# A hand-written order of the first units, written anew: which engine rounds which weight piece, and where each step stands

## The chip, the cores and the metric

One core of a Trainium2 chip. The metric is the device time of one execution in microseconds; the median of the runs is taken. The core's engines are TensorE (PE in the profile, PEld its weight loads), VectorE (DVE), ScalarE (ACT), GpSimd (POOL) and SyncE (SP), which issues most DMAs. Each runs its own instructions in the order in which the kernel wrote them and waits on semaphores for the others.

## The reference

A gated linear recurrence over 768 steps (4 batches, 8 heads, 48 features), and behind it a feed-forward layer with the maximum of three products:

```python
f = 1.0 / (1.0 + np.exp(-f_logit))
for t in range(S):
    state = f[:, :, t, :, None] * state + np.einsum('bhd,bhe->bhde', k[:, :, t], v[:, :, t])
    y[:, :, t] = np.einsum('bhd,bhde->bhe', q[:, :, t], state)
...
x = np.ascontiguousarray(attn_out.transpose(0, 2, 1, 3)).reshape(B * S, H * D)
h = np.maximum(np.maximum(x @ w1, x @ w2), x @ w3)
return (h @ w_out).astype(np.float32)
```

x is 3072 x 384; w1, w2 and w3 are 384 x 768, w_out is 768 x 384. The weights come as float64.

## The kernel before, in words

**Units.** The recurrence is cut into chunks of 64 steps. A unit is one chunk of two batches, all heads: 128 tokens, 24 units in all. Four units make a group of 512 tokens, for which the feed-forward layer then runs, as filler work on TensorE between the steps of later units. Units 0 to 3 and most of 4 and 5 go by the list of steps this case is about; from there on a loop issues them.

**One unit, by the names of the list** (the number behind a name is the unit): sT transposes the gates' logits on TensorE (L302), sA takes their sigmoid on ScalarE (L1039), s scans them backward on VectorE (L340, and a reciprocal, L343). kT transposes k, kM multiplies it by the scan (kh, VectorE, L1044). pS is the forward scan (L1051), qT and qM the same for q (qh, L1056). KT and KC turn kh back and copy it out (ks; L1062 on TensorE, L1065 on ScalarE). pP makes the scores within the chunk (a, L1072), pM masks them (L1076). v multiplies them by the values (y, L422), yP adds the part from the carried state (L1083, L1088), yC copies y out (o, L1093, ScalarE). SP makes the sums for the next state (L1102), SN adds them to it (L457 on ScalarE for units 0 and 1, L459 on VectorE behind that), c and kE scale and keep it on GpSimd. xP and xC turn the outputs into the layer's input xT (L1109, L1110). LD and LV load a unit's tensors.

**Weights.** They arrive as 24 pieces of 128 x 384 (LW loads so many; DMA at L222): piece n < 18 is column block j = n // 3 of w1, w2 or w3 by n % 3, the last six are w_out. Each piece is rounded from float64 to float32 in three steps. RB (`round_begin`) runs on ScalarE: the low word's part (rest_bits, L248) and, unless the piece is in BY_VECTOR, two activations that prepare the sign (top_bits, L244 and L245). RM (`round_merge`) runs on VectorE: one instruction (L262), or for a piece in BY_VECTOR two (a tensor_scalar at L259 and L260). RA (`round_add`) adds both parts on GpSimd (L269). top_bits has four buffers and rest_bits three, so RB of a piece waits for RA of the piece three before it.

**Differences.** w2 and w3 are replaced by w2 - w1 and w3 - w1 (`apart`, L766): AP n does it for piece n on GpSimd, AV n on VectorE. A product needs its piece's difference.

**The layer in the list.** F issues a product on TensorE (three matrix products into a bank, L553; 256 columns wide for the first twelve, 512 behind that, where it takes two F), E what takes it out of the bank: for w2 a copy on ScalarE (hm, L822), for w3 the maximum on VectorE (L824). There are two such banks (p). A bank is also taken by the transposes kT and qT of units 0 to 2, by yP's one-column product, by TP and by B (a filler product). TP j turns a piece of w1 on TensorE (L1115), TC j copies it back (L1117).

**What sets the order.** HEAD is a string of such steps. Each engine gets its instructions in the order of the string; nothing reorders them. So moving a step moves it on its own engine, and moves its place among the banks and buffers that it takes.

Of the kernel before, what the change touches and what calls it, by code (L numbers as in the profile page):

```python
# [55 lines left out]
def kernel(  # L56
# [33 lines left out]
    def fast():  # L90
        ctx = ExitStack()
        with ctx:
# [133 lines left out]
            def words(n):  # L226
                w = raw[n].rearrange("p (c two) -> p c two", two=2)
                return w[:, :, 0], w[:, :, 1]
# [2 lines left out]

            BY_VECTOR = (2, 3, 7, 9, 10, 12, 13, 15, 17)
            tops = keep.tile([128, 4, PIECE], FP32, name="top_bits")
            rests = keep.tile([128, 3, PIECE], FP32, name="rest_bits")

            def round_begin(n):
                if n in raw:
                    lo, hi = words(n)  # L240
                    top = tops[:, n % 4].bitcast(U32)
                    if n not in BY_VECTOR:

# [11 lines left out]
            def round_merge(n):  # L255
                if n in raw:
                    (top, rest), (_, hi) = halfway[n], words(n)
                    if n in BY_VECTOR:
                        nc.vector.tensor_scalar(top, hi, 3, 0x3FFFFFF8, op0=ALU.logical_shift_left, op1=ALU.bitwise_and)  # L259
# [757 lines left out]
            with tc.manual_schedule():  # L1017
# [11 lines left out]
                load_weights(6)  # L1029
                load_v(3)  # L1030
                xT = x_tiles[0]
                HEAD = """sT0 sA0 kT0 sT1 s0 kM0 kE0 kT1 qT0 pS0 sA1 s1 qM0 sT2 pP0 kM1 KT0 LD4 sA2 KT1 qT1 KC0 pS1 pM0 KC1 SP0 v0 qM1 SN0 pP1 kE1 s2 pM1 kT2 yP0 qT2 RB0 kE2 yC0 kM2 sT3 sA3 LW2 v1 RB1 KT2 KC2 LV4 c2 xP0 pS2 SP1 qM2 RB2 RM0 RM1 SN1 RA0 xC0 s3 RM2 pP2 RA1 B1 yP1 kT3 AP1 yC1 xP1 kM3 KT3 xC1 RB3 KC3 pS3 LW2 B1 kE3 F pM2 RM3 RB4 RA2 RM4 RA3 E qT3 v2 SP2 RB5 RB6 qM3 RA4 SN2 RB7 c3 AV2 AV4 pP3 yP2 RM5 F RM6 pM3 yC2 E RA5 RM7 F LW2 AV5 xP2 RA6 v3 LW2 xC2 TP0 SP3 E RB8 F RA7 AP7 TC0 SN3 RM8 LD5 TP1 E RB9 sT4 sA4 RA8 yP3 RM9 LV5 TC1 yC3 F AV8 kT4 xP3 E xC3 RA9 s4 RB10 kE4 TP2 kM4 F TC2 c4 RM10 E RB11 RB12 qT4 F RA10 LW2 RM11 E pS4 RA11 LW2 F RB13 E RM12 F qM4 RM13 E RB14 RA12 F RM14 E KT4 KC4 RB15 RA13 AP13 LW2 sT5 F RB16 LD6 E sA5 AV10 AV11 F LW2 E pP4 RA14 F RM15 RB17 F AV14 RA15 s5 kT5 RM17 LV6 pS5 TP3 RM16 qT5 RB18 RM18 LW2 E LW2 LW2 LW2 kE5 RA16 TC3 RA17 F F kM5 E RB19 LW2 c5 RA18 pM4 LW2 qM5 F AP16 S6"""
                BUDGET = -1146.666666666667
                held = {}
                first = ffn_first(xT)
# [84 lines left out]
                def RA(n):  # L1120
# [7 lines left out]
                           F=lambda n: next(first), E=lambda n: next(first))  # L1128
                for step in HEAD.split():
                    name = step.rstrip("0123456789")  # L1130
# [102 lines left out]
    def general():  # L1233
# [5 lines left out]
        with ctx:  # L1239
# [194 lines left out]
            for u in range(NU):  # L1434
# [5 lines left out]
                if u % GRP == GRP - 1:  # L1440
                    ffn(u // GRP, xT)

    fast()
    n_low = nc.values_load(low[0:1, 0:1], min_val=0, max_val=256)

# [32 lines left out]
```

## Time and profile before

| | us |
|---|---|
| median of 3 runs | 404.47 (404.35 to 405.72) |
| the profiled execution | 404.57 |
| its span, first to last instruction | 402.9 |
| TensorE busy | 388.4 |
| VectorE busy | 302.2 |
| GpSimd busy | 249.4 |
| ScalarE busy | 175.2 |

A row of the timeline gives an instruction's start and its length in us, the engine, the line, the operation, what it writes and reads, and in brackets how long the engine sat idle before and who ended that. TensorE executes one matrix product as two instructions, so a product F of three shows as x6. Instructions that follow each other overlap a little at their ends: a step of 0.68 is followed by the next after about 0.6.

### The profile page before, as it was taken

The page shows a single profiled execution, that of the slowest core. Times are in us where ns is not written, and L with a number is a line of the kernel's source. Part 1 is how long each engine was busy: PE and PEld are TensorE (multiplying, and loading weights), DVE is VectorE, ACT ScalarE, POOL GpSimd, SP SyncE. Part 2 cuts the span into 40 slices and gives each one's busy share as a digit, 9 for nine tenths or more (in the row PEclk, how much of TensorE's full clock was granted, in tenths as well). Part 3 has the DMA queues.
Part 4 walks back from the last instruction along what each step waited for, and adds up shares of the span by engine and source line. Part 5 has one row for each costly group of instructions (what it writes and reads, how often), then busy time and mean ns, then how long its engine had stood idle before and what let it go on. Part 6 is the DMA issues. An engine that isn't in the chain of part 4 may idle for free.

```text
span 402.9 us, 11666 instructions
## 1 busy us (share of the span) xinstructions
PE 388.4 (96%) x4658; PEld 339.2 (84%) x4658; DVE 302.2 (75%) x582; ACT 175.2 (43%) x419; POOL 249.4 (62%) x279
## 2 busy tenths in 40 slices
PE   4879999999999999999999999999999999999995
PEld 3768855569998889998889988899988899988995
DVE  6998998999989998997998997998995450002600
ACT  2675666513234432345532444523355325586120
POOL 2176546889997697296677277657477850535700
PEclk9999999999999999999999999999999999999999
DMA  8999886867564776676645476734572003452002
GB/s 166 238 298 278 208 236 81 193 88 125 97 94 90 112 146 145 115 112 83 123 122 92 65 115 86 167 68 80 79 158 86 0 19 92 129 146 70 2 20 63
DMA packets 181610, 47.21 MB, mean 117 GB/s; under 512 B 160496, under 2 KB 179248, under 8 KB 181552
## 3 DMA queue, kind: packets, MB, share of 16 engines
q1 hardware_dynamic: 177536, 45.52, 55.3%
q10 hardware_dynamic: 4016, 0.91, 1.1%
q8 instruction: 37, 0.61, 0.6%
q14 instruction: 21, 0.17, 0.1%
HBM read 37.75 MB, written 4.72 MB: 105 GB/s over the span
## 4 chain that ended last, share of the span: by engine, by line
PE 90%; DVE 3%; SPq 3%; DMA 2%; ACT 1%; issue 1%; POOL 0%; POOLq 0%
PE p L900 20%; PE p L640 18%; PE tr L900 16%; PE tr L640 14%; PE p L553 6%; PE y L426 3%; PE p L800 3%; PE y L515 2%; PE a L407 2%; PE a L444 2%; SPq L178 1%; SPq L164 1%; DMA raw<-in_moe_w_dram 1%; DMA placed<-in_moe_w_dram 1%; PE y L422 1%
## 5 line engine op out<-in xcount | busy, mean ns | idle before, releaser
L393 DVE STREAM_TRANSPOSE ks<-kh 32x128 f32<-32x128 f32 x256 | 77.4, 302 | 11.5 <-POOL kh L351 7.4
L900 PE MATMUL tr<-xT,placed 128*128 128x256 f32 x180 | 44.4, 384 | 0.0
L900 PEld LDWEIGHTS tr<-xT,placed 128*128 128x128 f32 x180 | 33.5, 190 | 4.9
L351 POOL TENSOR_TENSOR kh<-kt,r 128x512 f32<-128x512 f32 x18 | 31.9, 1772 | 8.5 <-DVE kt L307 8.5
L340 DVE TENSOR_TENSOR_SCAN r<-gate,from_one 128x520 f32<-128x520 f32 x24 | 35.1, 1463 | 2.6 <-issue 1.9
L553 PE MATMUL p<-xT,w_in 128*128 128x256 f32 (+1 forms) x108 | 33.7, 457 | 0.3 <-DVE hm L824 0.2
L604 POOL TENSOR_TENSOR w_in<-hm 128x256 f32<-128x256 f32 x18 | 13.3, 736 | 32.2 <-DVE hm L951 29.4
L522 ACT COPY xT<-y 64x256 f32<-64x256 f32 (+1 forms) x60 | 22.1, 369 | 22.4 <-PE y L515 21.6
L269 POOL TENSOR_TENSOR w_in<-top_bits,rest_bits 128x384 uint32<-128x384 uint32 x18 | 21.4, 1199 | 16.4 <-DVE top_bits L260 8.4
L900 PE MATMUL tr<-xT,w_in 128*128 128x256 f32 x120 | 30.8, 379 | 0.0
L648 DVE TENSOR_TENSOR o<-tr,w_in 128x384 f32<-128x384 f32 (+1 forms) x11 | 5.7, 521 | 33.4 <-PE tr L640 29.0
L900 PE MATMUL p<-w_in,placed 128*128 128x256 f32 x120 | 30.4, 382 | 0.0
L640 PE MATMUL p<-placed,hm 128*128 128x192 f32 x144 | 29.7, 332 | 0.0
L900 PE MATMUL p<-xT,placed 128*128 128x256 f32 x120 | 29.2, 379 | 0.0
L640 PE MATMUL tr<-w_out,w_in 128*128 128x192 f32 x144 | 28.6, 326 | 0.0
L350 POOL COPY ends<-r 128x8 f32<-128x8 f32 x18 | 6.7, 371 | 34.4 <-DVE r L340 34.4
L553 PEld LDWEIGHTS p<-xT,w_in 128*128 128x128 f32 x108 | 19.6, 190 | 9.5 <-issue 6.7
L943 DVE TENSOR_TENSOR hm<-tr,hm 128x512 f32<-128x512 f32 x15 | 10.3, 684 | 22.8 <-PE tr L900 15.9
L900 PEld LDWEIGHTS p<-w_in,placed 128*128 128x128 f32 x120 | 22.4, 190 | 4.4 <-issue 1.6
L291 ACT ACTIVATE raw<-top_bits 128x384 f32<-128x384 f32 x48 | 25.2, 526 | 0.4
L900 PEld LDWEIGHTS tr<-xT,w_in 128*128 128x128 f32 x120 | 22.8, 190 | 3.1
L900 PEld LDWEIGHTS p<-xT,placed 128*128 128x128 f32 x120 | 22.7, 190 | 2.8
(183 smaller groups left out, 980.1 us busy)
## 6 DMA issues: line engine op xcount, KB each, us to landing
raw<-in_moe_w_dram SPq DMA_DIRECT2D x24, 384.0 KB, 4.5
v_ld<-in_v_dram SPq DMA_DIRECT2D x48, 96.0 KB, 3.1
placed<-in_moe_w_dram SPq DMA_DIRECT2D x12, 384.0 KB, 5.9
out_dram<-o SPq DMA_DIRECT2D x45, 96.0 KB, 2.2
placed<-in_moe_w_out_dram SPq DMA_DIRECT2D x6, 384.0 KB, 5.3
f_ld<-in_f_logit_dram SPq DMA_DIRECT2D x36, 64.0 KB, 2.6
k_ld<-in_k_dram SPq DMA_DIRECT2D x36, 64.0 KB, 2.6
q_ld<-in_q_dram SPq DMA_DIRECT2D x36, 64.0 KB, 2.6
```

The source lines that it names most:

```text
L269: nc.gpsimd.tensor_tensor(dst, by(top), by(rest), op=ALU.add)
L291: nc.scalar.activation(over, size, AF.Relu, scale=(-1 / HI_MIN, 1.0)[step - 1], bias=(1.0, -HI_END * (1 - 2.0 ** -24))[step - 1], accum_ou ...
L340: nc.vector.tensor_tensor_scan(r[:, 0:LEN][:, ::-1], flat(gate)[:, ::-1], flat(from_one)[:, ::-1], 1.0, op0=ALU.mult, op1=ALU.max)
L351: (nc.vector if u < BY_ROWS else nc.gpsimd).tensor_tensor(kh.rearrange("p h a t -> p a h t"), kt, by_batch(r[:, 1:LEN + 1].rearrange("p (x ...
L393: nc.vector.transpose(ks[n * 32:(n + 1) * 32, :, par, e0:e0 + 32], kh[p0:p0 + 32, :, a, t0:t0 + 32])
L426: nc.tensor.matmul(y[o:o + DP, a, hp * C:(hp + 1) * C], lhsT=v_ld[s, 2 * hp + par, :], rhs=d["at"][s, par, hp, :], start=(hp == 0), stop=F ...
L522: nc.scalar.copy(xT[o, :, t0 + a * C:t0 + (a + 1) * C], y[i, a, 0:HP * C].rearrange("p (h t) -> p h t", h=HP))
L553: nc.tensor.matmul(p if w < TOK else p.rearrange("p (two t) -> p two t", two=2), lhsT=w_in[i][:, kt, j * 128:(j + 1) * 128], rhs=x[:, t.st ...
L604: engine.tensor_tensor(dst, x, y, op=op)
L640: nc.tensor.matmul(b[:, p * HD:(p + 1) * HD], lhsT=x, rhs=w, start=id(b) not in begun, stop=True, skip_group_check=True)
L800: nc.tensor.matmul(p[:, 0:DM], lhsT=w_in[0][:, a, j * 128:(j + 1) * 128], rhs=w_out[:, j, :], start=(j == 0), stop=(j == NJ - 1))
L900: nc.tensor.matmul(b[:, j * HALF:(j + 1) * HALF], lhsT=w[:, (2 * n + j) * 128:(2 * n + j + 1) * 128], rhs=x, start=begin and j == 0, stop= ...
```

## The change

BY_VECTOR, the pieces that VectorE rounds alone, is 1, 7, 10 and 17 in place of nine others, and HEAD is written anew. The diff, with the beginning of the two strings:

```diff
-            BY_VECTOR = (2, 3, 7, 9, 10, 12, 13, 15, 17)
+            BY_VECTOR = (1, 7, 10, 17)
...
-                HEAD = """sT0 sA0 kT0 sT1 s0 kM0 kE0 kT1 qT0 pS0 sA1 s1 qM0 sT2 pP0 kM1 KT0 LD4 sA2 KT1 qT1 KC0 pS1 pM0 KC1 SP0 v0 qM1 SN0 pP1 kE1 s2 pM1 kT2 yP0 qT2 RB0 kE2 yC0 kM2 sT3 sA3 ...
+                HEAD = """sT0 sA0 kT0 s0 kM0 pS0 sT1 sA1 kE0 s1 kT1 kM1 qT0 qM0 pS1 sT2 KT0 pP0 LD4 KC0 qT1 pM0 SP0 sA2 qM1 SN0 kE1 LW2 v0 pP1 s2 pM1 yP0 kT2 yC0 RB0 kM2 kE2 pS2 KT1 KC1 sT3 RB1 KT2 ...
```

Both strings hold the same steps of units 0 to 5, the same products and the same roundings. Of the differences, the old string has 1, 7, 13 and 16 on GpSimd and 2, 4, 5, 8, 10, 11 and 14 on VectorE; the new one has piece 2 on GpSimd (AP2) and the other ten on VectorE. On SyncE the loads of unit 5 (LD5) now stand ahead of pieces 15 and 16, and the last piece of w_out stands ahead of unit 6's loads. Behind the list every engine's order is as it was.

VectorE, from kh of unit 2 on (kh with r_103) to kh of unit 3 (r_104). Before:

```order
L1044 TENSOR_TENSOR kh<-p,r_103 128x2x4x64
L1051 SCALAR_TENSOR_TENSOR prod<-gate_99,from_inv_95 128x520
L1056 TENSOR_TENSOR qh<-p,prod 128x512
L262 SCALAR_TENSOR_TENSOR top_bits<-raw,top_bits 128x384 x2
L340 SCALAR_TENSOR_TENSOR r_104<-gate_100,from_one 128x520
L343 RECIPROCAL from_inv_97<-r_104 128x8
L259 TENSOR_SCALAR top_bits<-raw 128x384
L260 SCALAR_TENSOR_TENSOR top_bits<-raw,top_bits 128x384
L1044 TENSOR_TENSOR kh<-tr,r_104 128x2x4x64
```

And in the changed kernel, up to the first difference (w_in_64 holds w2, w_in_63 holds w1):

```order
L1044 TENSOR_TENSOR kh<-p,r_103 128x2x4x64
L1051 SCALAR_TENSOR_TENSOR prod<-gate_99,from_inv_95 128x520
L262 SCALAR_TENSOR_TENSOR top_bits<-raw,top_bits 128x384
L259 TENSOR_SCALAR top_bits<-raw 128x384
L260 SCALAR_TENSOR_TENSOR top_bits<-raw,top_bits 128x384
L340 SCALAR_TENSOR_TENSOR r_104<-gate_100,from_one 128x520
L343 RECIPROCAL from_inv_97<-r_104 128x8
L1056 TENSOR_TENSOR qh<-p,prod 128x512
L262 SCALAR_TENSOR_TENSOR top_bits<-raw,top_bits 128x384
L1044 TENSOR_TENSOR kh<-tr,r_104 128x2x4x64
L766 TENSOR_TENSOR w_in_64<-w_in_64,w_in_63 128x3x128
```

The tensor_scalar is now piece 1's, not piece 2's, the roundings of pieces 0 and 1 stand ahead of qh of unit 2, and the difference of piece 1 follows on this engine.

TensorE around the first product (w_in_64 is w2, w_in_65 is w3). Before, from the turning of unit 1's outputs on:

```order
L1109 MATMUL tr<-ident,o 128x128 x3
L1062 MATMUL tr<-ident,kh 128x128 x4
L1004 MATMUL p<-from_one,ident 128x256
L553 MATMUL p<-xT_146,w_in_64 128x256 x3
L302 MATMUL tr<-ident,q_ld_119 128x64x2 x4
L422 MATMUL y<-v_ld_128,at 64x48 x16
L1102 MATMUL a<-v_ld_128,ks 64x48 x16
L1072 MATMUL a<-qh,kh 64x64 x16
L1083 MATMUL p<-st_141 1x1
L1088 MATMUL y<-state,qh 64x48 x16
L553 MATMUL p<-xT_146,w_in_65 128x256 x3
```

And in the changed kernel, from the scores of unit 2 on:

```order
L1072 MATMUL a<-qh,kh 64x64 x16
L302 MATMUL tr<-ident,q_ld_119 128x64x2 x4
L1062 MATMUL tr<-ident,kh 128x128 x4
L553 MATMUL p<-xT_146,w_in_64 128x256 x3
L422 MATMUL y<-v_ld_128,at 64x48 x16
L1102 MATMUL a<-v_ld_128,ks 64x48 x16
L553 MATMUL p<-xT_146,w_in_65 128x256 x3
L1083 MATMUL p<-st_141 1x1
L1088 MATMUL y<-state,qh 64x48 x16
L1115 MATMUL p<-ident,w_in_63 128x128 x3
L1072 MATMUL a<-qh,kh 64x64 x16
L553 MATMUL p<-xT_146,w_in_64 128x256 x3
```

The transposes of q for unit 3 stand ahead of the first product, the second product stands between the sums of unit 2 and what reads the new state, and a piece of w1 is turned (L1115) ahead of the scores of unit 3.

ScalarE around the copy that empties the first product's bank (L822). Before, and then in the changed kernel:

```order
L248 ACTIVATE rest_bits<-placed_134 128x384
L1065 COPY ks<-tr 128x512
L244 ACTIVATE top_bits<-placed_134 128x384
L245 ACTIVATE top_bits<-top_bits 128x384
L248 ACTIVATE rest_bits<-placed_134 128x384
L822 COPY hm<-p 128x256
```

```order
L244 ACTIVATE top_bits<-placed_134 128x384
L245 ACTIVATE top_bits<-top_bits 128x384
L248 ACTIVATE rest_bits<-placed_134 128x384
L244 ACTIVATE top_bits<-placed_134 128x384
L245 ACTIVATE top_bits<-top_bits 128x384
L248 ACTIVATE rest_bits<-placed_134 128x384
L822 COPY hm<-p 128x256
```

Piece 3 is no longer rounded by VectorE, so both pieces 3 and 4 have three activations each ahead of the copy, where it was one and three.

More of the change, by code (lines that the diff above doesn't have):

```diff
@@ L1031, in fast @@
                 xT = x_tiles[0]
-                HEAD = """sT0 sA0 kT0 sT1 s0 kM0 kE0 kT1 qT0 pS0 sA1 s1 qM0 sT2 pP0 kM1 KT0 LD4 sA2 KT1 qT1 KC0 pS1 pM0 KC1 SP0 v0 qM1 SN0 pP1 kE1 s2 pM1 kT2 yP0 qT2 RB0 kE2 yC0 kM2 sT3 sA3 LW2 v1 RB1 KT2 KC2 LV4 c2 xP0 pS2 SP1 qM2 RB2 RM0 RM1 SN1 RA0 xC0 s3 RM2 pP2 RA1 B1 yP1 kT3 AP1 yC1 xP1 kM3 KT3 xC1 RB3 KC3 pS3 LW2 B1 kE3 F pM2 RM3 RB4 RA2 RM4 RA3 E qT3 v2 SP2 RB5 RB6 qM3 RA4 SN2 RB7 c3 AV2 AV4 pP3 yP2 RM5 F RM6 pM3 yC2 E RA5 RM7 F LW2 AV5 xP2 RA6 v3 LW2 xC2 TP0 SP3 E RB8 F RA7 AP7 TC0 SN3 RM8 LD5 TP1 E RB9 sT4 sA4 RA8 yP3 RM9 LV5 TC1 yC3 F AV8 kT4 xP3 E xC3 RA9 s4 RB10 kE4 TP2 kM4 F TC2 c4 RM10 E RB11 RB12 qT4 F RA10 LW2 RM11 E pS4 RA11 LW2 F RB13 E RM12 F qM4 RM13 E RB14 RA12 F RM14 E KT4 KC4 RB15 RA13 AP13 LW2 sT5 F RB16 LD6 E sA5 AV10 AV11 F LW2 E pP4 RA14 F RM15 RB17 F AV14 RA15 s5 kT5 RM17 LV6 pS5 TP3 RM16 qT5 RB18 RM18 LW2 E LW2 LW2 LW2 kE5 RA16 TC3 RA17 F F kM5 E RB19 LW2 c5 RA18 pM4 LW2 qM5 F AP16 S6"""
+                HEAD = """sT0 sA0 kT0 s0 kM0 pS0 sT1 sA1 kE0 s1 kT1 kM1 qT0 qM0 pS1 sT2 KT0 pP0 LD4 KC0 qT1 pM0 SP0 sA2 qM1 SN0 kE1 LW2 v0 pP1 s2 pM1 yP0 kT2 yC0 RB0 kM2 kE2 pS2 KT1 KC1 sT3 RB1 KT2 RM0 SP1 sA3 qT2 KC2 RM1 LV4 xP0 xC0 v1 s3 qM2 yP1 RB2 yC1 c2 RA0 B1 kT3 SN1 RM2 B1 xP1 kM3 RA1 xC1 AV1 pP2 pM2 pS3 RA2 qT3 KT3 RB3 RM3 F RB4 E RB5 RM4 v2 SP2 LW2 SN2 AP2 RA3 RA4 F yP2 KC3 yC2 kE3 RB6 qM3 RM5 AV4 E TP0 pP3 F RB7 RA5 pM3 RM6 RA6 TC0 RB8 E sT4 RM7 xP2 c3 xC2 v3 AV5 LW2 SP3 TP1 SN3 RM8 TC1 F RA7 RB9 AV7 LD5 yP3 LV5 sA4 LW2 E RA8 yC3 F AV8 RM9 E TP2 RB10 RM10 xP3 s4 F TC2 E RA9 kT4 xC3 pS4 RA10 kE4 F RB11 kM4 qT4 E F RM11 c4 RA11 E RB12 F RB13 RM12 E F LW2 AV11 E RB14 qM4 RM13 AV10 LW2 RA12 LW2 KT4 RM14 F E RA13 sT5 KC4 F TP3 LW2 RA14 AV13 LD6 E sA5 RB15 kT5 s5 kE5 LV6 qT5 RM15 F TC3 RB16 LW2 RB17 F RA15 AV14 E RB18 pS5 RM17 RM18 LW2 pP4 RM16 F RA16 RB19 pM4 kM5 F LW2 RA17 E c5 RA18 F S6 AV16 LW2 LW2 LW2 qM5"""
                 BUDGET = -1146.666666666667
```

## The prediction

> **What bounds the kernel now.** I read the page first, then the table of windows, then TensorE's timeline and the chain of waits over the first 64 us, where the change lies. The page gives the span, the busy times, and VectorE's busy tenths over 40 slices of 10.07 us:
>
> ```profile
> span 402.9 us, 11666 instructions
> PE 388.4 (96%) x4658; PEld 339.2 (84%) x4658; DVE 302.2 (75%) x582; ACT 175.2 (43%) x419; POOL 249.4 (62%) x279
> DVE  6998998999989998997998997998995450002600
> ```
>
> TensorE is busy 96% of the span and idle for 402.9 - 388.4 = 14.5 us. VectorE's 75% is an average: up to slice 30 it is nearly full, so early on two engines are close to the bound. The windows cut the early part where the two orders differ (25 to 63.53 us) and what follows (columns: length; then PE, PEld, DVE, ACT, POOL busy with counts; clock, DMA share, GB/s):
>
> ```profile
> 25.00:63.53 38.53, 37.44 (x408) 28.55 (x409) 36.73 (x56) 24.95 (x54) 22.84 (x23) 1.00 0.89 235
> 63.53:85.00 21.47, 21.47 (x309) 12.79 (x308) 19.98 (x37) 11.62 (x27) 17.30 (x15) 1.00 0.73 132
> ```
>
> Behind 63.53 us TensorE has no idle time, so the work there takes what it takes, and the end moves by what TensorE gains or loses ahead of it. TensorE's timeline shows its waits and the landmarks (brackets: idle time before, and who ended it):
>
> ```profile
> 25.10 0.66 PE L1062 MATMUL tr<-ident,kh 128*128 128x128 f32 x4 [1.24 <-DVE kh L1044]
> ...
> 26.02 1.46 PE L553 MATMUL p<-xT,w_in 128*128 128x256 f32 x6
> ...
> 30.17 0.69 PE L1072 MATMUL a<-qh,kh 48*64 48x64 f32 x32 [0.69 <-DVE st L459]
> ...
> 31.52 2.86 PE L553 MATMUL p<-xT,w_in 128*128 128x256 f32 x12
> ...
> 58.11 5.42 PE L553 MATMUL p<-xT,w_in 128*128 128x512 f32 x12
> ```
>
> The first feed-forward product (a step F) starts at 26.02. The two rows behind 31.52 are the second and third products; a product of 256 columns lasts 1.30 (a row below), so the third starts at 32.82. At 58.11 starts the first product from which the old and the new order on TensorE are the same. So three landmarks: 26.02, 32.82, 58.11.
>
> **The change part by part: what moves between engines.** Six pieces (2, 3, 9, 12, 13, 15) leave VectorE's rounding and one (1) enters. A piece that leaves drops one tensor_scalar on VectorE and gains two activations on ScalarE. Groups of 16 to 64 us, and GpSimd's differences (busy, mean ns):
>
> ```profile
> L259 DVE TENSOR_SCALAR top_bits<-placed 128x384 uint32<-128x384 uint32 x6 | 4.3, 713 | 0.0
> L259 DVE TENSOR_SCALAR top_bits<-raw 128x384 uint32<-128x384 uint32 x3 | 2.5, 827 | 0.0
> L766 DVE TENSOR_TENSOR w_in<-w_in,w_in 128x384 f32<-128x384 f32 x7 | 5.9, 860 | 0.0
> L766 POOL TENSOR_TENSOR w_in<-w_in,w_in 128x384 f32<-128x384 f32 x4 | 5.1, 1287 | 0.2
> ```
>
> VectorE loses 5 x (4.3 + 2.5) / 9 = 3.8 us and gains three differences, 3 x 0.84 = 2.5: a net 1.3 less. GpSimd loses 3 x 1.29 = 3.9. ScalarE's rows give the price of the two activations:
>
> ```profile
> 16.17 0.58 ACT L244 ACTIVATE top_bits<-raw 128x384 f32<-128x384 f32 x1 [1.15 <-DMA raw<-in_moe_w_dram]
> 16.78 0.53 ACT L245 ACTIVATE top_bits<-top_bits 128x384 f32<-128x384 f32 x1
> 17.21 0.53 ACT L248 ACTIVATE rest_bits<-raw 128x384 uint32<-128x384 uint32 x1
> 17.64 0.46 ACT L1093 COPY o<-y 128x384 f32<-128x384 f32 x1
> ```
>
> From 16.17 to 17.21 is 1.04 us a piece, so ScalarE gains 5 x 1.04 = 5.2. In the window from 25 us on it is busy 24.95 of 38.53, so this fits by the sum.
>
> **Up to the first product.** Up to 16.55 us the orders differ by two swaps (qh before kh, a transpose of kh) that leave VectorE's chain whole. VectorE's rows from there, and GpSimd's roundings:
>
> ```profile
> 16.55 0.68 DVE L1044 TENSOR_TENSOR kh<-p,r 128x512 f32<-128x512 f32 x1
> 17.14 1.23 DVE L1051 TENSOR_TENSOR_SCAN prod<-gate,from_inv 128x520 f32<-128x520 f32 x1
> ...
> 20.11 2.04 DVE L340 TENSOR_TENSOR_SCAN r<-gate,from_one 128x520 f32<-128x520 f32 x1
> 22.18 0.21 DVE L343 RECIPROCAL from_inv<-r 128x8 f32<-128x8 f32 x1
> ...
> 24.36 0.68 DVE L1044 TENSOR_TENSOR kh<-tr,r 128x512 f32<-128x512 f32 x1
> ...
> 27.19 0.34 DVE L259 TENSOR_SCALAR top_bits<-placed 128x384 uint32<-128x384 uint32 x1
> ...
> 29.55 0.56 DVE L459 TENSOR_TENSOR st<-a,state 128x384 f32<-128x384 f32 x1 [0.36 <-PE a L1102]
> 30.03 1.91 DVE L766 TENSOR_TENSOR w_in<-w_in,w_in 128x384 f32<-128x384 f32 x2
> ...
> 35.43 0.55 DVE L766 TENSOR_TENSOR w_in<-w_in,w_in 128x384 f32<-128x384 f32 x1
> ...
> 36.99 0.56 DVE L459 TENSOR_TENSOR st<-a,state 128x384 f32<-128x384 f32 x1 [1.01 <-PE a L1102]
> ...
> 63.53 0.70 DVE L307 STREAM_TRANSPOSE gate<-sig 128x512 f32<-128x512 f32 x1
> ```
>
> ```profile
> 19.78 3.16 POOL L269 TENSOR_TENSOR w_in<-top_bits,rest_bits 128x384 uint32<-128x384 uint32 x2 [3.15 <-DVE top_bits L262]
> ...
> 24.59 1.00 POOL L269 TENSOR_TENSOR w_in<-top_bits,rest_bits 128x384 uint32<-128x384 uint32 x1
> ```
>
> The same scan takes 1.23 or 2.04 and a difference 0.55 or, for two, 1.91: the long ones stand where GpSimd works, and GpSimd's two roundings beside that scan took 3.16 in place of 2 x 1.00. The two engines hold each other up, so each of GpSimd's roundings may cost VectorE up to 1.00 when they meet. The new path on VectorE: the scan of 17.14 ends at 18.4, the merge of piece 0 (0.5) at 18.9, tensor_scalar and merge of piece 1 with GpSimd's rounding of piece 0 between them (0.34 + 0.5 + 1.00) at 20.7, scan and reciprocal (1.23 + 0.21) at 22.1, qh (0.6, as kh from 16.55 to 17.14) at 22.7, merge of piece 2 (0.5) 23.2, kh (0.6) 23.8, and the difference of piece 1 (0.55), behind GpSimd's rounding of piece 2 (1.00 from 23.2), at 24.8. The first product then starts at 25.0, not 26.02. If neither rounding met VectorE it would be 23.5 by this path; if one more met it, 26.0. I take 25.0, since VectorE's rows beside roundings were long. The old order did the transposes of q for unit 3 (0.44) behind the first product, the new one ahead of it: a lead of 1.02 + 0.44 = 1.46 in work.
>
> **Up to the third product.** Work on TensorE, from the chain of waits (start, us, what):
>
> ```profile
> 27.48 0.44 PE tr L302 x4
> ...
> 34.38 0.33 PE tr L1109 x3
> 34.71 1.10 PE y L422 x32
> ...
> 36.29 0.61 PE a L1102 x32
> ...
> 39.16 0.12 PE p L1083 x2
> 39.27 0.61 PE y L1088 x32
> ...
> 42.47 1.30 PE p L553 x6
> ```
>
> Behind 25.0 stand the first product 1.30, the values of unit 2 (1.10), its sums 0.61, the second product 1.30, yP2 0.12 + 0.61, the turned piece TP0 0.33 and pP3 (about 0.61, as the sums): 5.98, to 30.98. The wait of 0.69 for the state (30.17) goes, since the second product stands in it. What comes late instead is TP0: it takes the bank of the second product, which VectorE frees behind state, qh, a merge and a difference (0.56 + 0.6 + 0.55 + 0.55 from 28.1, then the maximum over 256 columns, 0.4 as an estimate from kh's 0.68 over 512): 30.8 against 30.1 when TensorE is there, 0.7 more. Taking 0.5, the third product starts at 31.5, not 32.82, with TP0 (0.33) done: a lead of 1.65.
>
> **Up to 58.11.** From 32.82 on the old order does ten products of 256 columns (13.0), one of 512 (twice 1.30), v3 1.10, yP3 0.73, the sums of unit 3 and pP4 1.22, seven transposes of four (sT, kT and qT of units 4 and 5 and KT4: 3.1) and six of three (xP2, xP3 and four turned pieces: 2.0). That is 23.8 of 25.3, so 1.5 us are lost in small waits. If the new order loses as much, the lead stays at 1.65; if nothing, it is 3.2. VectorE decides. From the state row on (29.55, in the new order at about 28.2: 1.35 ahead) both orders do the merges of pieces 5 to 18. The new one does 3 tensor_scalars, not 8 (-5 x 0.75 = -3.8), two differences more (+1.7) and one qh more (+0.6): 1.5 less at mean durations. At undisturbed ones (0.34 and 0.55) it is 1.7 - 1.1 - 0.6 = 0. The idle 1.01 of row 36.99, where VectorE waits for TensorE's sums, goes with TensorE ahead. So at 63.53 VectorE leads by 1.35 to 3.9, TensorE by 1.65 to 3.2. Whichever is less counts; I take 2.3, that is 1.35 and the idle 1.0, with the disturbed part at its lower end, because GpSimd still does all its roundings.
>
> **The sum.** The profiled execution took 404.57, the median of the runs is 404.47 (404.35 to 405.72), 0.1 less. 404.57 - 2.3 = 402.27, so 402.2 for the median. Its own range, 1.35 to 3.2 gained, is 401.3 to 403.1. What hides the 5.2 us on ScalarE is its free time; if that cover went, see the last rival. On SyncE the one weight piece now ahead of unit 6's loads costs 0.4. Those loads come close:
>
> ```profile
> 62.84 5.60 SPq L187 DMA_DIRECT2D q_ld<-in_q_dram  x8
> ```
>
> ```profile
> 72.95 0.68 DVE L307 STREAM_TRANSPOSE qt<-q_ld 128x512 f32<-128x512 f32 x1
> ```
>
> The last q load is issued by 68.44 and used at 72.95; used 2.3 earlier it has 2.2 left to land. If SyncE's queue stays where it was, VectorE waits some tenths there, which TensorE need not see.
>
> **The rivals.** *Given back at the shared access (404.2).* Each added difference reads two inputs in SBUF. If each first waits out a rounding of GpSimd, the three cost 3 x 1.55 = 4.7 in place of 2.5, and 2.1 of the 2.3 are gone: 404.47 - 0.2 = about 404.2. For it: the pair of 1.91. Against: the single ones of 0.55, and three GpSimd differences of 1.29 that no longer hold VectorE. The Trainium skill, GPSIMD Engine Reference, Specifications, says that GpSimd's SBUF interfaces are shared with VectorE, with contention for instructions in a two-port mode or with two SBUF inputs. By that rule differences moved to VectorE do not run beside GpSimd; the trace agrees where a scan of 1.23 took 2.04. The sum by that rule is this rival's 404.2, by the mean of the differences' rows 402.2.
>
> *Slower: ScalarE's order (407.4).* It is in order, and two activations more (1.04) may stand ahead of the hm copy that frees a bank for the next product but one. The first product's copy now stands behind the rounds of pieces 3 and 4. If each of the five net pieces holds a product up for its full 1.04, TensorE loses 5.2, and 404.5 - 2.3 + 5.2 = 407.4. It decides once a copy starts over 1.30 (a product) behind its product's end. Against: ScalarE has 13.6 us free between 25 and 63.53 and gets 5.2.
>
> *More than forecast (400.6).* GpSimd's 3.9 less also frees VectorE, and the lead passes 3.2, to 4 at most by VectorE's 3.9. *The change does less than it says:* four differences (1, 7, 13, 16) go to VectorE, but that of piece 2 goes to GpSimd, so ten of eleven stand on VectorE; the three net ones of the sums.
>
> **How the numbers follow.** Forecast 0.57, given back 0.27, slower 0.12, more than forecast 0.04. About 0.5% (2.0 us) is what a measurement of this kernel can tell from no change. Of the forecast, 0.40 lies above 2.0 gained: faster 0.40 + 0.04 = 0.44. Same: 0.17 + 0.27 and 0.01 of the slower rival where it costs little: 0.45. Slower 0.11. The range from 401.0 to 405.0 leaves out the slower case and the largest gains, some 0.17.
>
> **What would show it.** Right: the first product at 24.5 to 25.7, the third at 31 to 32, the first of 512 columns behind pP4 at 55 to 56.5, gate<-sig on VectorE at 60.5 to 62, and the rest shifted as a block. Wrong: hm copies on ScalarE late by over a product; VectorE's differences at 1 us or more each; a wait of TensorE behind 63 us that was not there; or the lead present at 60 us and gone at 398.

## The result, and the profile after

Both kernels were timed in turn on one chip: the changed one took 401.86 us in the median (401.34 to 402.75, 6 runs), the one before 405.01 (404.35 to 406.91, 6 runs). The ratio is 0.9919 with a 95% interval from 0.9901 to 0.9937 (it is estimated from all runs; the quotient of the medians is 0.9922), so the change makes the kernel faster by 0.6 to 1.0%. The runs of the kernel before lie in two groups, near 404.4 and near 405.7, so its median moves between 404.5 and 405.7 from one comparison to the next. The profiled execution of the changed kernel took 401.35, that of before 404.57: 3.2 less, as in the medians (3.15).

The head of the page of the changed kernel: span, busy times, and VectorE's busy tenths.

```profile
span 399.6 us, 11667 instructions
PE 388.7 (97%) x4658; PEld 339.5 (85%) x4658; DVE 297.5 (74%) x580; ACT 179.4 (45%) x429; POOL 245.8 (62%) x276
DVE  6998998999989998997998997998985450002600
```

TensorE's busy time is the same within 0.3 (388.4 before), and the span is 3.3 shorter: what went is idle time of TensorE. ScalarE gained 4.2 (10 activations), VectorE lost 4.7, GpSimd 3.6. The same two stretches in the windows, cut at the new place of `gate<-sig`, show where it was (columns as before):

```profile
25.00:60.90 35.90, 35.90 (x412) 27.27 (x415) 33.00 (x52) 29.17 (x64) 21.67 (x22) 1.00 0.94 259
60.90:82.37 21.47, 21.47 (x307) 12.75 (x300) 19.78 (x37) 11.58 (x28) 15.26 (x14) 1.00 0.67 115
```

From 25.00 on TensorE has no idle time (35.90 of 35.90), where it had 1.09 (37.44 of 38.53). The second stretch is as it was: 21.47 of 21.47 in both.

TensorE's timeline of the changed kernel, at the landmarks of the prediction:

```profile
24.94 1.46 PE L553 MATMUL p<-xT,w_in 128*128 128x256 f32 x6
...
27.90 1.56 PE L553 MATMUL p<-xT,w_in 128*128 128x256 f32 x6
29.39 0.19 PE L1083 MATMUL p<-st 128*1 128x1 f32 x2
29.51 0.68 PE L1088 MATMUL y<-state,qh 48*64 48x48 f32 x32
30.12 0.55 PE L1115 MATMUL p<-ident,w_in 128*128 128x128 f32 x3
...
31.23 1.56 PE L553 MATMUL p<-xT,w_in 128*128 128x256 f32 x6
...
47.48 1.46 PE L553 MATMUL p<-xT,w_in 128*128 128x256 f32 x6
48.78 0.60 PE L302 MATMUL tr<-ident,f_ld 128*128 128x128 f32 x4
...
55.01 5.42 PE L553 MATMUL p<-xT,w_in 128*128 128x512 f32 x12
...
71.74 1.45 PE L800 MATMUL p<-w_out,w_in 128*128 128x384 f32 x4
```

No row between 24.94 and 71.74 has a bracket: TensorE waits for nobody there. Three rows of before, two that show what else went besides the wait of 0.69 for the state, and the last landmark:

```profile
50.18 1.46 PE L553 MATMUL p<-xT,w_in 128*128 128x256 f32 x6
51.83 1.56 PE L553 MATMUL p<-xT,w_in 128*128 128x256 f32 x6 [0.19 <-DVE hm L824]
...
74.84 1.45 PE L800 MATMUL p<-w_out,w_in 128*128 128x384 f32 x4
```

From the start of a product to that of the next instruction it is 1.30 where nothing holds TensorE up (47.48 to 48.78 in the changed kernel). Before it was 1.65 at 50.18, because VectorE's maximum (L824) freed the bank late. Only 0.19 of these 0.35 is marked as a wait. The row itself is 1.46 long in both, and the other 0.16 is its end, which the next instruction overlaps when it need not wait.

VectorE's rows of the changed kernel, around the first product and at the end of the stretch:

```profile
18.79 0.35 DVE L259 TENSOR_SCALAR top_bits<-raw 128x384 uint32<-128x384 uint32 x1
19.17 1.26 DVE L260 SCALAR_TENSOR_TENSOR top_bits<-raw,top_bits 128x384 uint32<-128x384 uint32 x1
20.35 1.23 DVE L340 TENSOR_TENSOR_SCAN r<-gate,from_one 128x520 f32<-128x520 f32 x1
...
23.36 1.04 DVE L766 TENSOR_TENSOR w_in<-w_in,w_in 128x384 f32<-128x384 f32 x1
24.32 0.68 DVE L1076 TENSOR_TENSOR at<-a,mask 128x512 f32<-128x512 f32 x1
...
28.04 0.56 DVE L459 TENSOR_TENSOR st<-a,state 128x384 f32<-128x384 f32 x1 [0.76 <-PE a L1102]
...
30.05 0.41 DVE L824 SCALAR_TENSOR_TENSOR hm<-hm,p 128x256 f32<-128x256 f32 x1
31.36 0.69 DVE L1076 TENSOR_TENSOR at<-a,mask 128x512 f32<-128x512 f32 x1 [0.90 <-PE a L1072]
...
47.31 0.42 DVE L824 SCALAR_TENSOR_TENSOR hm<-hm,p 128x256 f32<-128x256 f32 x1 [0.51 <-PE p L553]
...
60.90 0.69 DVE L307 STREAM_TRANSPOSE gate<-sig 128x512 f32<-128x512 f32 x1
```

VectorE waits for TensorE three times here (0.76, 0.90 and 0.51), and TensorE never for VectorE.

| landmark | before | after | lead | forecast of after |
|---|---|---|---|---|
| first product | 26.02 | 24.94 | 1.08, and the transposes of q (0.44) done | 25.0 |
| third product | 32.82 | 31.23 | 1.59, and TP0 (0.33) done | 31.5 |
| first product of 512 behind pP4 | 58.11 | 55.01 | 3.10 | 55 to 56.5 |
| `gate<-sig` on VectorE | 63.53 | 60.90 | 2.63 | 60.5 to 62 |
| first product with w_out (L800) | 74.84 | 71.74 | 3.10 | |
| span | 402.9 | 399.6 | 3.3 | |

### The profile page after: what moved, and what is told of

The parts are those of the page before. It is cut to its first block, busy times and chain, and to the rows that moved or that the text cites. A ratio compares the mean times of both kernels' runs of the same rounds, so it can differ in the third digit from the quotient of the medians.

```text
span 399.6 us, 11667 instructions
## 1 busy us (share of the span) xinstructions
PE 388.7 (97%) x4658; PEld 339.5 (85%) x4658; DVE 297.5 (74%) x580; ACT 179.4 (45%) x429; POOL 245.8 (62%) x276
## 4 chain that ended last, share of the span: by engine, by line
PE 94%; SPq 3%; DMA 1%; ACT 0%; issue 0%; DVE 0%
PE p L900 20%; PE p L640 18%; PE tr L900 17%; PE tr L640 14%; PE p L553 8%; PE y L426 3%; PE p L800 3%; PE y L515 2%; PE a L407 2%; PE a L444 2%; SPq L178 1%; DMA raw<-in_moe_w_dram 1%; SPq L164 1%; PE tr L302 1%; PE y L422 1%; PE a L1072 0%
## 5 line engine op out<-in xcount | busy, mean ns | idle before, releaser
L340 DVE TENSOR_TENSOR_SCAN r<-gate,from_one 128x520 f32<-128x520 f32 x24 | 33.0, 1374 | 2.6 <-issue 2.0
```

The costliest lines, as they stand in the source:

```text
L340: nc.vector.tensor_tensor_scan(r[:, 0:LEN][:, ::-1], flat(gate)[:, ::-1], flat(from_one)[:, ::-1], 1.0, op0=ALU.mult, op1=ALU.max)
```

## The experiments

Twelve kernels, each timed against the kernel before on the chip of its group. The intervals are about 0.2% to either side, 0.8 us, so a difference of that size between two of them is read from the profiles and not from the medians. In the edits, "the new list" is the changed kernel and "the old list" the one before.

**1. The new roundings alone, in the old list.**

```diff
-            BY_VECTOR = (2, 3, 7, 9, 10, 12, 13, 15, 17)
+            BY_VECTOR = (1, 7, 10, 17)
```

> The old list with its differences where they were, and only the set of pieces that VectorE rounds alone taken from the change (1, 7, 10, 17). Theory (the order makes the gain, by the first product coming 1.1 us earlier and the second product filling the state's wait; the lighter VectorE is only room for it): VectorE does 3.8 us less, but TensorE had lost just 1.5 us in small waits behind the third product, and the first product stays at 25.5 to 26.1 us; 0.3 to 1.5 us gained, ratio to before 0.996 to 0.999. Rival (the rounding set is the gain): 2.5 to 3.3 us gained, ratio 0.992 to 0.994.

405.86 in the median against 404.54, ratio 1.0022 (1.0005 to 1.004). In its profile the first product stands at 26.16 (26.02 before) and the first of 512 behind pP4 at 57.94 (58.11), with `gate<-sig` at 62.81, 0.7 ahead. The relief of VectorE alone gains nothing, and neither the theory's range nor the rival's came in. The scan is short here too (1.23, at 21.00), but the first product is not earlier for it: at 22.68 TensorE has waited 1.83 (0.92 before) for the copy of unit 1's new state, which stands on ScalarE behind the three activations of piece 2 (20.72 to 22.17), where there was one.

**2. The new list with the old nine pieces on VectorE.**

```diff
-            BY_VECTOR = (1, 7, 10, 17)
+            BY_VECTOR = (2, 3, 7, 9, 10, 12, 13, 15, 17)
```

> The new list, differences where the change has them, with the old set of nine pieces rounded by VectorE alone. Theory: the first product still at 25.0 +/- 0.5 and the third at 31 to 32 us, so the lead of some 1.7 us at the third product stays; behind it VectorE, with 3.8 us more, takes part of the rest back: 1 to 2.3 us gained, ratio 0.9945 to 0.9975. Rival (the rounding set is the gain): nothing gained or a loss, 0.999 or more. Rival (the order alone, and VectorE never decides): the full 3 us, 0.991 to 0.993.

402.22, ratio 0.9933 (0.9906 to 0.9959). The first and the third product stand where the changed kernel has them (24.93 and 31.21), `gate<-sig` at 61.96, 1.06 late. One wait for a maximum comes back on TensorE:

```profile
52.06 2.41 PE L553 MATMUL p<-xT,w_in 128*128 128x512 f32 x5 [0.20 <-DVE hm L824]
```

The first product of 512 behind pP4 comes at 55.45 in place of 55.01. So 1.06 us of lateness on VectorE cost TensorE 0.44. The order, with its differences on the engines that it was written for, carries nearly the whole gain: the ratio lies between the theory's range and that of the second rival.

**3. Five differences moved, in the old list.** Steps AP1, AP7, AP13, AP16 and AV2 of the old list as AV1, AV7, AV13, AV16 and AP2.

> The old list and the old rounding set; at their places in the list the differences of pieces 1, 7, 13 and 16 go from GpSimd to VectorE and that of piece 2 to GpSimd. Theory: VectorE gets 2.5 us more in a list where it is already full, GpSimd 3.9 less, which holds VectorE less; 0.4 us gained to 1 lost, ratio 0.999 to 1.0025. Rival (the differences are the gain, since GpSimd's 1.29 us each hold VectorE up): 1.5 to 3 us gained, 0.9925 to 0.996.

405.86, ratio 1.0016 (0.9995 to 1.0037): no gain, as the theory had it. Its profiled execution took 407.07, well over its median, and is not read for sizes; it does show a new wait, of TensorE at 32.82 for the difference of piece 2, which comes late on GpSimd in this order.

**4. The same five put back, in the new list.**

> The changed kernel with the differences back where the old list had them: pieces 1, 7, 13 and 16 on GpSimd and piece 2 on VectorE, at the same places in the list. Theory: the first product keeps its start within 0.3 us of 24.94, because the transposes of kh ahead of it end as late; later GpSimd's chain is longer by 3.9 us and some product waits for it: 0.2 to 1.2 us of the gain lost, ratio to before 0.9925 to 0.9955. Rival (the differences are the gain): all lost, 0.998 or more.

403.37, ratio 0.9961 (0.9938 to 0.9983). The first product keeps its place (24.86), the second comes at 29.30 in place of 27.90. The table of TensorE's waits names who was late (us in total, times, longest):

```profile
PE p L553 <- DVE w_in L766: 1.4, 1, 1.4
```

That is the difference of piece 2, now on VectorE. By the ratio 1.7 us of the gain are lost, more than the theory's 0.2 to 1.2, and the loss starts at the second product, not at a later one behind GpSimd's chain. Experiments 6 and 10 take the five apart.

**5. The second product behind yP2 again, in the new list.**

```diff
-... SN2 AP2 RA3 RA4 F yP2 KC3 yC2 kE3 RB6 qM3 RM5 AV4 E TP0 ...
+... SN2 AP2 RA3 RA4 yP2 KC3 yC2 kE3 RB6 qM3 RM5 AV4 F E TP0 ...
```

> The changed kernel with one step moved: the second product stands behind yP2 again, where the old order had it, so nothing stands on TensorE between the sums of unit 2 and what reads the new state. Theory (the product fills the wait for the state): sums end at 27.9, the state row stands at 28.04 and lasts 0.56, so TensorE waits 0.7 there, the third product starts at 31.9 to 32.0 in place of 31.23, and the loss stays to the end: about 402.6, ratio to the kernel before 0.994, span about 400.3. Rival (the wait would be made up for behind it, since small waits absorb it): the third product at 31.9, the first of 512 columns behind pP4 still at 55.0, ratio 0.992.

402.95, ratio 0.9939 (0.9918 to 0.996). TensorE's rows:

```profile
28.71 0.19 PE L1083 MATMUL p<-st 128*1 128x1 f32 x2 [0.94 <-DVE st L459]
...
29.44 1.56 PE L553 MATMUL p<-xT,w_in 128*128 128x256 f32 x6
...
31.89 1.56 PE L553 MATMUL p<-xT,w_in 128*128 128x256 f32 x6
```

The wait for the state is back with 0.94, and the third product comes 0.66 later, though the first was 0.20 earlier (24.74). At 55 us the loss is still 0.65 (55.66). Behind that, in this execution, TensorE waited 0.96 more at 64.66 for a copy on ScalarE, behind a sigmoid that waited 1.39 for unit 6's logits. The product does fill the wait for the state, and what it saves is not made up for later.

**6. The difference of piece 2 on VectorE, in the new list** (AP2 as AV2; then all eleven stand on VectorE).

> The changed kernel with the difference of piece 2 on VectorE at the place in the list where it stood on GpSimd; the other ten stay on VectorE. Theory (the loss of the run with five differences put back is all the second product's wait for piece 2's difference): the second product at 29.3 in place of 27.9, 403.3 to 403.5, ratio 0.996, as in that run. Rival (the four differences put back on GpSimd cost that run most of it): the second product at 28.0, ratio 0.992 to 0.993.

403.73, ratio 0.9968 (0.9952 to 0.9985). VectorE's row of that difference, and TensorE's row of the second product:

```profile
28.70 0.79 DVE L766 TENSOR_TENSOR w_in<-w_in,w_in 128x384 f32<-128x384 f32 x1
```

```profile
29.55 1.56 PE L553 MATMUL p<-xT,w_in 128*128 128x256 f32 x6 [1.39 <-DVE w_in L766]
```

On VectorE the difference stands in order behind the new state, which waits for the very sums behind which the second product is to run. On GpSimd it is done by 25.27 (24.06 and 1.21, in the changed kernel). The 1.39 stays to the end: the third product comes 1.64 late (0.19 of it from the first product on), the span is 1.7 longer.

**7. No piece rounded by VectorE, in the new list** (BY_VECTOR empty).

> The changed kernel with no piece rounded by VectorE alone: four tensor_scalars (about 0.35 to 0.8 each, 1.4 to 3.2 in all) leave VectorE, and eight activations (4 x 1.04 = 4.2) come to ScalarE. Theory (VectorE does not decide behind the first product, and ScalarE has free time): 401.5 to 402.3, ratio 0.991 to 0.993; the first product may start some 0.3 to 0.5 earlier, since piece 1's tensor_scalar stands ahead of it, if ScalarE prepares piece 1 in time. Rival 1 (VectorE decides): up to 2 us faster, ratio 0.987. Rival 2 (ScalarE's order): copies late, ratio above 0.996.

402.62, ratio 0.9939 (0.992 to 0.9959): VectorE does 2.2 us less than in the changed kernel (295.3 against 297.5), ScalarE 3.7 more, and the kernel is no faster; by its profile (span 400.6) it is 1.0 slower. The ratio lies between the theory's range and that of the second rival. ScalarE's and TensorE's rows:

```profile
35.37 0.36 ACT L822 COPY hm<-p 128x256 f32<-128x256 f32 x1
```

```profile
35.78 1.56 PE L553 MATMUL p<-xT,w_in 128*128 128x256 f32 x6 [0.21 <-ACT hm L822]
42.23 1.56 PE L553 MATMUL p<-xT,w_in 128*128 128x256 f32 x6 [0.20 <-ACT xT L1110]
```

The third product ended at 32.6 and its copy started at 35.37, 2.8 later, behind three roundings and a copy: the bank is late for the next product. This is the prediction's rival of ScalarE's order, one step further than the change goes.

**8. Fourteen pieces rounded by VectorE, in the new list** (BY_VECTOR 1 and 5 to 17).

> The changed kernel with fourteen pieces rounded by VectorE (1 and 5 to 17) in place of four: ten tensor_scalars more on VectorE (10 x 0.34 to 0.83, that is 3.4 to 8.3 us, before 64 us), twenty activations fewer on ScalarE (10.4 us). With nine pieces the loss was 0.4 of a median. Theory (VectorE's slack behind the third product is about 2 to 3 us, and only what goes beyond it is lost): gate<-sig at 63 to 65, TensorE waits for maxima between 45 and 60 us, about 403 to 405, ratio 0.995 to 1.000. Rival (VectorE does not decide at all before 64 us): 401.9 to 402.4, ratio 0.992 to 0.993.

404.03, ratio 0.998 (0.9969 to 0.9992). `gate<-sig` stands at 63.95, 3.05 late, and TensorE waits for maxima again:

```profile
46.74 1.56 PE L553 MATMUL p<-xT,w_in 128*128 128x256 f32 x6 [0.46 <-DVE hm L824]
...
53.66 0.70 PE L553 MATMUL p<-xT,w_in 128*128 128x512 f32 x1 [0.69 <-DVE hm L824]
```

The product behind pP4 comes at 57.06, 2.05 late. With 2: of 1.06 us of lateness on VectorE, read at `gate<-sig`, 0.44 went through to TensorE, of 3.05 then 2.05. So VectorE can come 0.6 to 1.0 us later there before TensorE pays for the rest. At a single place the slack can be less: in 2 the maximum ahead of the product of 512 is 0.66 late (51.59 against 50.93), and that product 0.35 (52.06 against 51.71).

**9. The old list without GpSimd's first two additions.**

```diff
-                    nc.gpsimd.tensor_tensor(dst, by(top), by(rest), op=ALU.add)
+                    if n in (0, 1):
+                        nc.gpsimd.tensor_tensor(dst[:, :, 0:2], by(top)[:, :, 0:2], by(rest)[:, :, 0:2], op=ALU.add)
+                    else:
+                        nc.gpsimd.tensor_tensor(dst, by(top), by(rest), op=ALU.add)
```

> The kernel before, with GpSimd's additions of pieces 0 and 1 cut from 384 columns to 6 (the rest of both pieces is set to 0.0 at the start, so the first columns of the layer are not the reference's): no GpSimd work of length stands beside VectorE's scan at 20.11. Theory (VectorE and GpSimd hold each other up, and this sets the first product): the scan takes 1.23 in place of 2.04, kh of unit 3 (24.36) comes 0.8 to 2 earlier, the first product starts at 24.2 to 25.2 in place of 26.02, and the median falls by about 1 us or less, as other waits follow: ratio 0.997 to 1.0. Rival (the long rows come from something else, such as a wait for data): the scan keeps its 2.04 and the first product its 26.0.

404.07 against 405.67, ratio 0.9967 (0.9948 to 0.9985). The profiled execution (405.82, well over its median) began late, because TensorE stayed at half speed until 15 us, and its scan starts at 21.83 in place of 20.11, so the first product's place (26.53) tells nothing. The lengths do. GpSimd and VectorE:

```profile
21.59 1.47 POOL L270 TENSOR_TENSOR w_in<-top_bits,rest_bits 128x6 uint32<-128x6 uint32 x2 [2.96 <-DVE top_bits L262]
23.14 1.00 POOL L771 TENSOR_TENSOR w_in<-w_in,w_in 128x384 f32<-128x384 f32 x1
```

```profile
21.83 1.23 DVE L345 TENSOR_TENSOR_SCAN r<-gate,from_one 128x520 f32<-128x520 f32 x1
...
23.22 1.13 DVE L259 TENSOR_SCALAR top_bits<-raw 128x384 uint32<-128x384 uint32 x1
```

Without a long addition beside it the scan takes 1.23 in place of 2.04, and the stretch from its start to kh is 3.03 (21.83 to 24.86) in place of 4.25 (20.11 to 24.36). The hold-up is real, and in the old list it cost VectorE about 1.2 us ahead of the first product; the ratio fits that (0.3%, 1.3 us, by its interval 0.6 to 2.1). It works both ways: the second of the short additions begins at 22.06, beside the scan, and ends only with it at 23.06. GpSimd's difference then meets the tensor_scalar, which takes 1.13 in place of 0.34.

**10. Four differences on GpSimd again, in the new list** (AP1, AP7, AP13, AP16; AP2 stays).

> The changed kernel with the differences of pieces 1, 7, 13 and 16 on GpSimd again at the same places of the list; that of piece 2 stays on GpSimd. Theory (the four moved differences bring nothing, and the loss of the run with five put back was all the difference of piece 2): second product at 27.8 to 28.0, 401.6 to 402.2, ratio 0.991 to 0.993. Rival (they free GpSimd's chain or save a hold-up): 402.5 to 403.5, ratio 0.994 to 0.996.

403.0, ratio 0.9955 (0.9939 to 0.9971): the theory fell, the rival held. The second and third product are on time (28.17 and 31.50, 0.27 late as the first was). The loss comes between 46 and 50 us. GpSimd's, VectorE's and TensorE's rows there:

```profile
46.09 2.09 POOL L269 TENSOR_TENSOR w_in<-top_bits,rest_bits 128x384 uint32<-128x384 uint32 x2 [0.95 <-ACT top_bits L245]
```

```profile
47.24 1.35 DVE L766 TENSOR_TENSOR w_in<-w_in,w_in 128x384 f32<-128x384 f32 x1 [0.89 <-POOL w_in L269]
48.52 0.41 DVE L824 SCALAR_TENSOR_TENSOR hm<-hm,p 128x256 f32<-128x256 f32 x1
```

```profile
49.62 0.63 PE L302 MATMUL tr<-ident,f_ld 128*128 128x128 f32 x4 [0.39 <-PE p L553]
```

GpSimd, later by the differences it does again, rounds a piece late; VectorE waits 0.89 in order for that piece, and the maximum behind it is 1.2 later than in the changed kernel (48.52 against 47.31). The product behind stands 0.88 late at 50.09, where the one ahead was 0.29 late (47.77 against 47.48). So the four differences on VectorE are worth about 0.6 here, by way of GpSimd's chain. The loss then grows in steps, to 1.3 with a wait of 0.22 for a copy on ScalarE at 64.32, and from 1.5 to 2.1 with a wait of 0.41 for a maximum at 153.77. Whether the moved differences cause these later waits is not settled. Against the changed kernel experiments 6 and 10 cost 2.0 and 1.5 by their ratios, and 4 (both together) 1.7, each with some 0.8 to either side: they do not add up. The trace of 4 shows why in part: TensorE is 1.40 late from the second product on and still 1.40 at the first of 512 behind pP4 (56.41), so what GpSimd's chain costs at 46 to 50 us in 10 is covered there by the earlier wait.

**11 and 12. Products of the identity ahead of the first transposes, in the new list**, twelve and then five: to see whether a version faster than both is to be had. TensorE's rows before 20 us show why it was tried: in each profiled execution a transpose of 128 columns lasts 0.42 at first and 0.27 from some point between 9.1 and 15.2 us on, another point each time.

```diff
+                def W(n):
+                    p = bank()
+                    for _ in range(n):
+                        nc.tensor.matmul(p[:, 0:128], lhsT=ident, rhs=ident, start=True, stop=True)
...
-                HEAD = """sT0 sA0 kT0 s0 kM0 pS0
+                HEAD = """W12 sT0 sA0 kT0 s0 kM0 pS0
```

> The changed kernel with twelve products of the identity with itself (128 columns) on TensorE ahead of the first transposes, from about 1.7 to 4.4 us, where TensorE is idle; their result is not used. In the profiles so far a transpose lasts 0.42 up to some point between 9.2 and 15.2 us, another in each execution, and 0.27 from there on, and the runs of one kernel lie in two groups about 1.4 us apart. Theory (TensorE's full speed comes a while after it became busy, and when it comes sets the spread): full speed by 5 to 9 us, the first product 0.5 to 1.5 earlier than 24.94, the runs closer together, 400.5 to 401.3, ratio 0.988 to 0.990. Rival (VectorE's chain from 6 us on sets the first product, and the clock comes when it comes): 401.9, ratio 0.992.

405.26, ratio 1.0004 (0.9989 to 1.002), so it lost all the gain. TensorE's rows:

```profile
1.61 5.49 PE L1122 MATMUL p<-ident 128*128 128x128 f32 x24 [1.61 <-POOL ident masks.py:199]
6.89 1.06 PE L302 MATMUL tr<-ident,f_ld 128*128 128x128 f32 x4
7.74 0.64 PE L302 MATMUL p<-ident,k_ld 128*128 128x128 f32 x4
...
14.46 1.03 PE L1072 MATMUL a<-qh,kh 48*64 48x64 f32 x32 [2.15 <-DVE qh L1056]
15.42 1.11 PE L302 MATMUL p<-ident,q_ld 128*128 128x128 f32 x4
```

I had taken the products at half their length: they hold the first transposes until 6.89. Full speed is there at 7.74, and behind a wait of 2.15 it is gone again (a transpose of four in 1.11, and 0.64 before).

> As the run with twelve products ahead, with five: there the twelve took 5.3 us (0.44 each), held the first transposes from 4.5 to 6.9 us, and the first product of the layer came 3.35 late. Five take 2.2, from 1.6 to 3.8, and end before the transposes' data is there. Theory (full speed comes some us after TensorE became busy, and this sets the spread): full speed by about 8 us, the first product 0.3 to 1.0 earlier than 24.94, 400.8 to 401.5, ratio 0.989 to 0.991. Rival (TensorE falls back to half speed in its waits between 8 and 16 us, as it did with twelve, so an earlier start buys nothing): 401.5 to 403, ratio 0.992 to 0.995.

402.5, ratio 0.9939 (0.9913 to 0.9965), and the first product at 25.07: no gain. TensorE was busy from 1.61 and still at half speed to about 9:

```profile
4.25 1.08 PE L302 MATMUL tr<-ident,f_ld 128*128 128x128 f32 x4
...
9.08 0.68 PE L302 MATMUL p<-ident,q_ld 128*128 128x128 f32 x4
```

The rival's time came, but not its mechanism: behind 9.08 no row is at half speed again.

No kernel of the twelve beats the changed one.

## Why the prediction was right, and where it was off

**Up to the first product: right in time, and half right in its cause.** 24.94, forecast 25.0. The scan takes 1.23, since in the new order GpSimd's addition meets the merge L260 (1.26) instead, and the difference takes 1.04 beside the next addition. Experiment 9 shows the hold-up by taking the additions away. But VectorE's path, which the prediction summed to 24.8, was done at 24.4 and did not set the product. TensorE came 0.5 later from its own work, in which it is without idle time from 18.17 on (6.77 of 6.77 us); the sum had left that work out. So that the two times lie so close is in part luck. Nor was VectorE's hold-up all that went: from 18 us to the first product TensorE had waited 1.24 for VectorE and 0.80 and 0.92 for ScalarE, and it now waits once, 0.77 for ScalarE. Experiment 1 shows the same from the other side.

**Up to the third product: right, slightly small.** 31.23, forecast 31.5; with TP0 done that is a lead of 1.92 for the 1.65 of the forecast. The wait of 0.69 for the state is gone because the second product fills it; experiment 5 brings it back with 0.94. TP0 did not come late by the 0.5 of the forecast: it follows yP2 at 30.12 without a wait, though VectorE's maximum ends only at 30.46. In experiments 2 and 8 it starts at 30.11 and 30.14, before the maximum (30.68 and 30.46) has begun. So TP0 does not wait for the bank that this maximum frees, and the term of 0.5 stood for a wait that is not there. That the difference of piece 2 went to GpSimd, which the prediction named only as a way in which the change does less, is what makes this step work: experiment 6 loses 1.39 without it.

**Up to 58.11: the step that was mis-sized.** The prediction said "VectorE decides" and "whichever is less counts; I take 2.3". TensorE's lead came out at 3.10, near the upper end of its term (3.2): of the 1.5 us lost in small waits behind the third product 1.2 went. VectorE's lead came out at 2.63, close to the 2.3, but it was not what counted. TensorE waits for nobody from 24.94 on, VectorE waits for TensorE, and experiments 2 and 8 show that VectorE can come 0.6 to 1.0 us later before TensorE pays. So the rule that the lesser lead counts was wrong here, and with it "VectorE decides".

That VectorE's 2.3 is so near the 2.63 is luck besides. From the state row to `gate<-sig` the prediction took off the idle 1.0 and left the work as it was. The windows of that stretch (29.55 to 63.53 before, 28.04 to 60.90 after) show the reverse: VectorE's idle time grew from 1.4 to 2.1, and its work fell from 32.6 to 30.7. The tensor_scalars went from 5.5 to 1.0 (from seven to three; the prediction counted eight). The 14 merges rose from 8.7 to 11.0, since it is now some of them that stand beside GpSimd's additions, as the one of 1.26 above. Nine differences took 5.8, where seven had taken 5.9. The group of differences from 16 to 64 us in the changed kernel (count, busy, mean ns):

```profile
L766 DVE TENSOR_TENSOR w_in<-w_in,w_in 128x384 f32<-128x384 f32 x11 | 7.4, 674 | 0.4 <-POOL w_in L269 0.4
```

The last of the eleven (63.71, 0.56) stands behind the list, and before it stood at 67.03. So the three that came to VectorE cost 0.9 in all (7.4 less 0.6 and less 5.9), not 2.5, and over the whole span VectorE does 4.7 us less, not 1.3.

So 0.9 of the gain was missing from the forecast, 2.3 for 3.2. The times themselves differ by only 0.3 (402.2 and 401.86), as the median of before was 405.01 in this comparison and 404.47 in the runs that the prediction had; that is chance.

**Behind the list: right.** The lead is 3.10 at 55.01, 3.10 at 71.74 and 3.3 in the span. The q loads that come close on SyncE cost nothing: VectorE's row, 3.10 ahead of its old place and without a wait:

```profile
69.85 0.68 DVE L307 STREAM_TRANSPOSE qt<-q_ld 128x512 f32<-128x512 f32 x1
```

SyncE's queue came forward too: the last of them is issued by 66.56, where it was 68.44. But unit 6's loads stand close in this order. In experiments 5 and 12 its logits came late, and TensorE waited 0.96 and 0.52 behind them.

**The rivals.** *Given back at the shared access* did not come: the differences became cheaper on the mean, and putting four of them back on GpSimd costs time (experiment 10). What was given back, the 2.3 us on the merges, is less than the 4.5 saved on the tensor_scalars. *ScalarE's order* is not seen in the changed kernel. The copies behind the first and the third product:

```profile
26.35 0.56 ACT L248 ACTIVATE rest_bits<-placed 128x384 uint32<-128x384 uint32 x1
26.81 0.36 ACT L822 COPY hm<-p 128x256 f32<-128x256 f32 x1
...
34.42 0.35 ACT L822 COPY hm<-p 128x256 f32<-128x256 f32 x1
```

The first starts 0.5 behind its product's end (26.3), the second 1.8 behind (32.6). That is over the 1.30 from which the prediction let this rival decide, and still TensorE did not wait, since 2.8 us of other work stands there between the products (32.63 to 35.44). So the point was set too low for this place.

With four pieces more on ScalarE it does appear (experiment 7: 2.8 behind the end, 0.2 of wait at two places, 1.0 in the span), so the price of the added work on ScalarE at nothing (5.2 us in the sum, 4.2 by the page) was right with little to spare. *More than forecast* gave GpSimd's lighter load as its cause. The gain did pass the forecast, but that cause is not shown: up to `gate<-sig` GpSimd was busy for 0.60 of the window (21.67 of 35.90) and before for 0.59 (22.84 of 38.53).

**What the experiments add.** Roundings and differences moved alone gain nothing in the old list (1 and 3). In the new one they carry part of the gain: the nine old roundings cost 0.4 us on TensorE's timeline, the four differences 0.6 by 50 us, that of piece 2 1.4. The gain belongs to the order together with the engines that it was made for, and not to one of the parts. The new order with the old roundings and the old differences at once was not run, so what the bare order is worth stays open.

## What to carry to other kernels

Put independent work of the bound engine into the wait between a result and the engine that turns it into the next operand, and see that this work's own input is made on an engine that does not stand in that very chain: here 1.4 us hung on where one subtraction was done. Before moving work between engines to relieve a busy one, ask how much of its lateness reaches the bound engine: here less than half of the first microsecond did, and most of what came beyond it. And read waits by the time from a row's start to the next row's start, beside that of an undisturbed row, and not by the brackets alone.

## What was not expected of the hardware

**Which instructions GpSimd holds up.** Beside GpSimd's work a VectorE instruction that reads two tensors in SBUF becomes longer (scan 1.23 to 2.04, merge 0.55 to 1.26, difference 0.55 to 1.04 and 1.18), and so does a tensor_scalar with one (0.34 to 1.13). The masking, which has one operand in a bank of products, does not: `at<-a,mask` took 0.68 at 24.32, beside GpSimd's difference from 24.06 to 25.27, and 0.66 to 0.69 elsewhere. The row of 0.34 is shorter than a merge of the same size (0.55). The Trainium skill, VectorE: DVE Perf Modes, Mode 2×_2P, tells of a mode in which an instruction with a single tensor input reads that tensor through both read ports; by that and by GPSIMD Engine Reference, Specifications, the tensor_scalar would be held up too, and the trace agrees with its 1.13.

**TensorE's speed at the start.** Half speed lasted until 9.1 to 15.2 us (7.7 in experiment 11, where it came back), another time in each execution, though TensorE started at 4.3 to 4.5 in all but the last two kernels; in experiment 9 that made the work at 16 us 1.8 to 2.0 late. The kernel's runs spread by 1.5 us and more (404.35 to 406.91 before). That this is the cause of the spread was not shown. The Trainium skill, TensorE: Matmul & The Clock Gate, Part 1, says that full speed follows a busy window of about 3.4 us, that the window runs freely, and that an idle one takes it back. The trace agrees in that the point changes from run to run. It does not agree in two things: in experiment 11 full speed was lost behind idle times of 1.52 and 2.15, each shorter than such a window, and in experiment 12 TensorE was busy for 2.5 of the first 2.6 us and most of the next five, and full speed came only at about 9.
